# Linear attention into a SwiGLU block on one core: inputs as (head half, 64 chunks of 9 tokens)

## The chip, the cores and the metric

The kernel runs on one core of one Trainium2 chip. The metric is the device time of one execution in microseconds (us). TensorE (PE) has a 128x128 array with a weight load (PEld) ahead of each matmul; VectorE is DVE, ScalarE is ACT, GpSimd is POOL, and SyncE (SP) only issues DMAs here. Each engine takes its own instructions in program order, so an instruction that waits holds up all that stands behind it on its engine.

## What is computed

```python
q, k, v: (8, 8, 576, 64) float32          # batch, heads, tokens, head dim
def phi(x): return np.where(x > 0, x, np.exp(x) - 1.0) + 1.0      # elu(x) + 1
q_p, k_p = phi(q), phi(k)
kv  = np.einsum('bhsd,bhse->bhde', k_p, v)
z   = np.sum(k_p, axis=2)
num = np.einsum('bhsd,bhde->bhse', q_p, kv)
den = np.einsum('bhsd,bhd->bhs', q_p, z)[..., None] + 1e-06
x   = (num / den).transpose(0, 2, 1, 3).reshape(4608, 512)
g   = x @ w_gate                          # 512 x 1536
out = (g * sigmoid(g)) * (x @ w_val) @ w_out   # 1536 x 512, float32 out
```

## The kernel before

The 4608 tokens go through the block in nine groups of 512. Groups 0 to 7 are the first 512 tokens of each batch entry ("batch" below); group 8 holds the last 64 tokens of all eight (the tails).

**Layout.** A batch's k, q and v come as tiles of 128 partitions x 8 heads x (4 tokens x 64) float32: token `4p + j` on partition p, so each contiguous run is 1 KB. The tails come in pairs, 64 partitions each, in runs of 256 bytes. `load` (L96) issues all of it on SP: one DMA of 1 MB per tensor, and for every even batch two tail DMAs more. The output leaves on SP too. The weights come on POOL, cast to float16 on the way.

**Attention of a batch.** exp on ACT (L117), then `min(e,1) + max(x,0)` on DVE (L130, L133). `vcast` (ACT, L168) copies v to float16 with a column of ones beside each head, so that `mm1` (L186: 4 pieces of 128 tokens and a tail piece, for 4 head pairs: 20 matmuls of 129 columns) gives kv and z at once. `kv_copies` writes the kv blocks to `R` and the z columns to diagonal matrices, `zb` (L209) spreads z over the partitions by a matmul with ones. `s3_prod`, `s3_reduce`, `s3_recip`, `s3_scale` (DVE) give the denominators and scale q; `tr` transposes q by head pairs on PE, DVE copies it to `qT`; `mm2` (L271) multiplies by `R` and gives `xT`, the block's input.

**The block of a group.** `l1(g, fb)` for 12 slices of 128 hidden channels: 4 matmuls into `pG`, 4 into `pV` (512 columns each), Silu on ACT (L290), product on DVE (L291) into `hT`. Then `l2(g, t)` for 4 token pieces: 12 matmuls each into `pO`, evacuated, stored. `pG`, `pV`, `pO` and `pA` have two banks each.

**Order.** `manual_schedule`: the order on each engine is that of the code. Group g's l1 slices carry, by the table `chain`, the attention of batch g+1, and its l2 pieces, by `prep_a`, the exp and phi of batch g+2. The cast of v of batch g+2 stands at slices 4 to 7. Group 0 is different: the whole of batch 1 (`ch[8]` to `ch[11]`, then `pa`) and the phi of batch 2 go through in it. The loads of batch g+2 are issued at slice 0 of group g, behind the stores of group g-1 on SP.

```python
            if 4 <= fb < 8 and b2 < B:
                vcast(b2, [fb - 4])
```

Of the kernel before, what the change touches and what calls it, by code (L numbers as in the profile page):

```python
# [17 lines left out]
def kernel(  # L18
# [42 lines left out]
    kp = two([P, J, H * D], FP16, "kp")
    qp = two([P, J, H * D], FP16, "qp")
    ktp = two([P, H * D], FP16, "ktp")
    qtp = two([P, H * D], FP16, "qtp")
    vm = two([P, J, H, D + 1], FP16, "vm")
    vt = [two([P, H, D + 1], FP16, f"vt{i}") for i in range(2)]
    prod = sb.tile([P, 2, H * D], FP16, name="prod")
    prodt = sb.tile([P, H * D], FP16, name="prodt")
    den = sb.tile([P, J * H], FP32, name="den")
    rden = sb.tile([P, J * H], FP32, name="rden")  # L70
    dent = sb.tile([P, H], FP32, name="dent")
    rdent = sb.tile([P, H], FP32, name="rdent")
    zd = sb.tile([P, NH2, P], FP16, name="zd")
    zbc = sb.tile([P, H * D], FP16, name="zbc")
    R = [sb.tile([P, NH2, P], FP16, name=f"R_{b}") for b in range(B)]
    qT = two([P, NH2, NM], FP16, "qT")
    qTt = sb.tile([P, NH2, NM], FP16, name="qTt")
    xT = [two([P, NM], FP16, f"xT{c}") for c in range(NH2)]
    hT = two([P, FB, NM], FP16, "hT")
    sil = two([P, NM], FP16, "sil", 2)  # L80
    osb = two([P, 2, DM], FP32, "osb")
    wg = sb.tile([P, NH2, DF], FP16, name="wg")
# [22 lines left out]
    def load_k(b):
        load(b, k, k32, kt32)

    def load_q(b):
        load(b, q, q32, qt32)

    def load_v(b):
        load(b, v, v32, vt32)


    def exps(src, srct, e, et, b):
        for i in range(2):
            nc.scalar.activation(out=e[:, 4 * i:4 * i + 4, :], in_=src[b % 2][:, 4 * i:4 * i + 4, :],  # L117
                                 func=AF.Exp, bias=0.0, scale=1.0)
# [353 lines left out]
```

## Time and profile before

| | us |
|---|---|
| three timed runs | 430.30, 430.93, 432.88 (median 430.93) |
| the profiled execution | 431.02 |
| span of its trace | 429.30 |
| PE busy | 332.6 (77%) |
| DVE busy | 240.4 (56%) |
| ACT busy | 168.9 (39%) |
| DMA packets | 45,494, of which 13,728 under 512 bytes and 29,184 more under 2 KB |
| granted TensorE clock, mean | 0.936 |

Matmuls overlap in the array, so a row's duration is its latency, and the price of a matmul in a stream is the distance from start to start. An engine's busy share is a mean over stages with different limits; the stages are read apart below.

### The profile page before, as it was taken

What the parts mean: (1) busy time and instruction counts of PE and PEld (TensorE: products, weight loads), DVE (VectorE), ACT (ScalarE), POOL (GpSimd) and SP (SyncE); (2) the same over time, 40 slices, a digit from 0 to 9 for tenths busy, and PEclk for the clock granted to TensorE, in tenths of its full rate; (3) what the DMA queues carried; (4) which work ended last, traced back from release to release, by engine and by line L of the source; (5) the groups of instructions that cost most, each with busy time, mean ns of one, the idle gap of its engine ahead of it and who ended that gap; (6) DMA issues with size and microseconds to landing.
All of it is one profiled execution on the core that took longest, in us unless ns stands there. A gap on an engine that the chain in (4) does not pass through costs nothing.

```text
span 429.3 us, 4508 instructions
## 1 busy us (share of the span) xinstructions
PE 332.6 (77%) x1672; PEld 154.6 (36%) x1672; DVE 240.4 (56%) x430; ACT 168.9 (39%) x271; POOL 10.5 (2%) x26
## 2 busy tenths in 40 slices
PE   0329506386788995699879948998799999999995
PEld 0113202142334452245334523453345444444442
DVE  3583102467978663678576626786666772342431
ACT  3604006752344741564346513744365221321320
POOL 3420000000000000000000000000000000000000
PEclk9999856888899999799999996999899999999999
DMA  8899992001630069004701780046002002002004
GB/s 234 184 247 247 240 273 43 1 0 50 214 128 2 1 211 253 2 0 148 246 2 43 205 219 0 0 158 234 0 20 82 2 0 99 0 2 98 0 2 98
DMA packets 45494, 42.76 MB, mean 100 GB/s; under 512 B 13728, under 2 KB 42912, under 8 KB 45472
## 3 DMA queue, kind: packets, MB, share of 16 engines
q1 hardware_dynamic: 40720, 37.75, 30.4%
q0 software_dynamic: 4752, 4.72, 6.5%
q8 instruction: 13, 0.21, 0.2%
q14 instruction: 9, 0.07, 0.1%
HBM read 37.75 MB, written 9.44 MB: 110 GB/s over the span
## 4 chain that ended last, share of the span: by engine, by line
PE 52%; DMA 16%; SPq 15%; DVE 9%; ACT 4%; issue 3%; DVEq 0%; POOL 0%; ACTq 0%; POOLq 0%
PE pO_137 L297 11%; PE pO_138 L297 10%; SPq L102 10%; DMA v_0_67<-in_v_dram 7%; PE pG_133 L287 7%; PE pG_134 L287 7%; PE pV_135 L287 7%; PE pV_136 L287 6%; DMA v_1_68<-in_v_dram 5%; SPq L97 5%; DMA q_0_65<-in_q_dram 2%; DVE qp_81 L231 2%; DVE qp_82 L231 2%; DMA k_1_64<-in_k_dram 1%; DVE hT_121 L291 1%
## 5 line engine op out<-in xcount | busy, mean ns | idle before, releaser
L287 PEld LDWEIGHTS <-wg 128*128 128x128 f16 x432 | 42.5, 101 | 86.1 <-issue 43.9
L287 PEld LDWEIGHTS <-wv 128*128 128x128 f16 x432 | 43.5, 101 | 55.1 <-issue 7.3
L291 DVE SCALAR_TENSOR_TENSOR hT_120<-pV_136,sil_123 128x512 f16<-128x512 f32 x30 | 20.7, 689 | 61.3 <-ACT sil_123 L290 48.1
L290 ACT ACTIVATE sil_122<-pG_133 128x512 f16<-128x512 f32 x54 | 32.2, 597 | 53.2 <-PE pG_133 L287 53.1
L290 ACT ACTIVATE sil_123<-pG_134 128x512 f16<-128x512 f32 x54 | 32.1, 595 | 41.2 <-PE pG_134 L287 38.8
L287 PE MATMUL pG_134<-xT_0_112,wg 128*128 128x512 f16 x30 | 12.2, 408 | 32.9 <-ACT sil_123 L290 32.9
L291 DVE SCALAR_TENSOR_TENSOR hT_120<-pV_135,sil_122 128x512 f16<-128x512 f32 x30 | 20.7, 689 | 24.7 <-PE pV_135 L287 20.5
L297 PEld LDWEIGHTS <-hT_120 128*128 128x128 f16 x240 | 23.7, 100 | 28.4 <-issue 2.3
L303 ACT ACTIVATE osb_125<-pO_138 128x512 f32<-128x512 f32 x9 | 5.4, 597 | 65.9 <-PE pO_138 L297 65.9
L297 PE MATMUL pO_137<-wo,hT_120 128*128 128x512 f16 x120 | 29.2, 396 | 0.0
L291 DVE SCALAR_TENSOR_TENSOR hT_121<-pV_136,sil_123 128x512 f16<-128x512 f32 x24 | 16.5, 689 | 22.1 <-ACT sil_123 L290 11.6
L297 PE MATMUL pO_138<-wo,hT_120 128*128 128x512 f16 x120 | 27.5, 379 | 0.0
L297 PEld LDWEIGHTS <-hT_121 128*128 128x128 f16 x192 | 18.8, 98 | 22.6
L168 ACT ACTIVATE vm_87<-v_0_67 128x512 f16<-128x512 f32 x16 | 9.7, 625 | 42.5 <-DMA v_0_67<-in_v_dram 42.5
L291 DVE SCALAR_TENSOR_TENSOR hT_121<-pV_135,sil_122 128x512 f16<-128x512 f32 x24 | 16.5, 689 | 17.2 <-PE pV_135 L287 15.2
L297 PE MATMUL pO_137<-wo,hT_121 128*128 128x512 f16 x96 | 22.0, 379 | 0.0
L297 PE MATMUL pO_138<-wo,hT_121 128*128 128x512 f16 x96 | 22.0, 379 | 0.0
L221 DVE TENSOR_REDUCE den<-prod 128x16 f32<-128x1024 f16 x16 | 19.4, 1211 | 0.1
L301 DVE TENSOR_SCALAR osb_124<-pO_137 128x512 f32<-128x512 f32 x9 | 6.2, 691 | 17.9 <-PE pO_137 L297 17.9
L186 PE MATMUL pA_139<-vm_87,kp_79 128*128 128x129 f16 x32 | 4.6, 251 | 14.4 <-DVE kp_79 L133 13.7
L168 ACT ACTIVATE vm_88<-v_1_68 128x512 f16<-128x512 f32 x16 | 9.7, 625 | 8.5 <-DMA v_1_68<-in_v_dram 8.5
L252 PE MATMUL pA_139<-id_130,qp_81 128*128 128x128 f16 x32 | 3.8, 254 | 11.4 <-DVE qp_81 L231 11.3
(207 smaller groups left out, 663.2 us busy)
## 6 DMA issues: line engine op xcount, KB each, us to landing
k_0_63<-in_k_dram SPq DMA_DIRECT2D x4, 1024.0 KB, 6.8
v_0_67<-in_v_dram SPq DMA_DIRECT2D x4, 1024.0 KB, 9.6
q_0_65<-in_q_dram SPq DMA_DIRECT2D x4, 1024.0 KB, 9.9
k_1_64<-in_k_dram SPq DMA_DIRECT2D x4, 1024.0 KB, 7.2
q_1_66<-in_q_dram SPq DMA_DIRECT2D x4, 1024.0 KB, 9.6
v_1_68<-in_v_dram SPq DMA_DIRECT2D x4, 1024.0 KB, 11.4
out_dram<-osb_124 SPq DMA_DIRECT2D x8, 512.0 KB, 2.7
out_dram<-osb_125 SPq DMA_DIRECT2D x8, 512.0 KB, 3.3
```

The lines of the kernel that those rows point to most:

```text
L97: nc.sync.dma_start(out=main[b % 2][:, :, :], in_=src[b][:, 0:NM, :].rearrange("h (p j) d -> p h (j d)", j=J))
L102: nc.sync.dma_start(out=tail[(b // 2) % 2][TL * e:TL * e + TL, :, :], in_=src[b + e][:, NM:S, :].rearrange("h p d -> p h d"))
L168: nc.scalar.activation(out=vm[b % 2][:, j, :, 0:D], in_=v32[b % 2][:, :, D * j:D * j + D], func=AF.Copy, bias=0.0, scale=1.0)
L186: nc.tensor.matmul(out=o, lhsT=kp[b % 2][:, j, P * hp:P * hp + P], rhs=vm[b % 2][:, j, :, :].rearrange("p h c -> p (h c)")[:, 130 * hp:130 ...
L221: nc.vector.tensor_reduce(out=den[:, cs], in_=prod[:, :, :].rearrange("p j (h d) -> p (j h) d", h=H), axis=AX.X, op=ALU.add)
L231: nc.vector.tensor_tensor(out=qv, in0=qv, in1=rden[:, H * j:H * j + H].unsqueeze(2).to_broadcast([P, H, D]), op=ALU.mult)
L287: nc.tensor.matmul(out=ps[:, :], lhsT=w[:, cc, P * fb:P * fb + P], rhs=xT[cc][g % 2][:, :], start=(cc == 0), stop=(cc == NH2 - 1))
L290: nc.scalar.activation(out=s[:, :], in_=pG[i][:, :], func=AF.Silu, bias=0.0, scale=1.0)
L291: nc.vector.scalar_tensor_tensor(out=hT[g % 2][:, fb, :], in0=pV[i][:, :], scalar=SC, in1=s[:, :], op0=ALU.mult, op1=ALU.mult)
L297: nc.tensor.matmul(out=ps[:, :], lhsT=hT[g % 2][:, fb, P * t:P * t + P], rhs=wo[:, fb, :], start=(fb == 0), stop=(fb == FB - 1))
L301: nc.vector.tensor_scalar(out=o[:, t % 2, :], in0=ps[:, :], scalar1=1.0 / SC, scalar2=None, op0=ALU.mult)
L303: nc.scalar.activation(out=o[:, t % 2, :], in_=ps[:, :], func=AF.Copy, bias=0.0, scale=1.0 / SC)
```

## The change

**Layout.** A batch's tile is now 128 partitions = 2 head halves x 64 chunks; on a partition lie 4 heads x 9 tokens x 64. The contiguous run is 9 x 64 x 4 = 2304 bytes, 64 x 9 = 576 leaves no rest, and all tail tiles and their work are gone. Every tensor comes in four DMAs of 295 KB: two head pairs x two halves, the half of partitions 0 to 63 on SP, that of 64 to 127 on POOL.

**Groups.** 72 units (batch, token of the chunk) of 64 tokens in nine groups of 8 units. Group g holds the last g units of batch g-1 and the first 8-g of batch g; group 8 is the rest of batch 7.

**kv.** The contraction runs over 64 partitions: per head pair, 9 tokens x 2 halves = 18 matmuls of 129 columns on 64 rows of the array each, halves in turn, each half into its own bank: 36 a batch for 20. For batches 0 to 2, z comes by 18 matmuls of 256 columns from kp directly (`z_direct`), so that the denominators don't wait for v; later batches keep the diagonal way (2 matmuls of 256).

**Order.** Three tables: `early` for batches 1 and 2 (in groups 0 and 1), `late` for batch 3, `steady` for 4 to 7. One batch per group throughout. Casts of v of batch g+2 stand at slices 8 and 9 from group 1 on; the loads of batch g+2 are written at slice 4. mm2 stands after or between the l2 pieces (before: slices 10 and 11).

**Silu.** In slices 0 to 3 of groups 0 and 1 the gate is 0.5·g·(1 + tanh(g/2)): Tanh on ACT and one more DVE instruction.

**Banks.** `pV` has three, the attention shares three (`pX`, in turn), l2 uses banks of pV and pG. The copy of the transposed q is on ACT. Stores are of 64 rows of 2 KB.

```diff
-        nc.sync.dma_start(
-            out=main[b % 2][:, :, :],
-            in_=src[b][:, 0:NM, :].rearrange("h (p j) d -> p h (j d)", j=J))
...
+        v4 = src[b].rearrange("(a l) (c j) d -> a c l (j d)", a=2, j=J)
+        for hh, eng in ((0, nc.sync), (1, nc.gpsimd)):
+            eng.dma_start(out=dst[b % 2][C * hh:C * hh + C, 2 * lp:2 * lp + 2, :],
+                          in_=v4[hh][:, 2 * lp:2 * lp + 2, :])
...
+        for j in range(J):
+            for hh in range(2):
+                rows = slice(C * hh, C * hh + C)
                 nc.tensor.matmul(
+                    out=kvb[b][hh][:, 256 * lp:256 * lp + W], lhsT=kp[b % 2][rows, j, P * lp:P * lp + P],
+                    rhs=vm[b % 2][rows, j, :, :].rearrange("p l c -> p (l c)")[:, 130 * lp:130 * lp + W],
+                    start=(j == 0), stop=(j == J - 1))
...
+    def z_direct(b):
+        zps[b] = (bank(), bank())
+        for j in range(J):
+            for hh in range(2):
+                rows = slice(C * hh, C * hh + C)
+                nc.tensor.matmul(out=zps[b][hh][rows, 0:HL * D], lhsT=ones[rows, 0:C], rhs=kp[b % 2][rows, j, :],
+                                 start=(j == 0), stop=(j == J - 1))
...
+        if tanh:
+            nc.scalar.activation(out=s[:, :], in_=pg[:, :], func=AF.Tanh, bias=0.0, scale=0.5)
+            nc.vector.scalar_tensor_tensor(out=s[:, :], in0=s[:, :], scalar=1.0, in1=pg[:, :],
+                                           op0=ALU.add, op1=ALU.mult)
...
+    def early(b):
...
+        sl[0] = [lambda: exp_k(b, 0)]
+        sl[1] = [lambda: exp_k(b, 1)]
+        sl[2] = [lambda: exp_q(b, 0)]
+        sl[3] = [lambda: exp_q(b, 1)]
+        sl[4] = [lambda: phi_k(b, 0)]
+        sl[6] = [lambda: phi_k(b, 1)]
+        sl[7] = [lambda: z_direct(b)]
+        sl[8] = [lambda: phi_q(b, 0)]
+        sl[10] = [lambda: phi_q(b, 1)]
+        sl[11] = s3a(b, 0)
...
+    def steady(b):
...
+        sl[0] = [lambda: phi_q(b, 0), lambda: mm1(b, 0)]
+        sl[1] = [lambda: phi_q(b, 1), lambda: mm1(b, 1)]
+        sl[2] = [lambda: zdiag(b, 0), lambda: zdiag(b, 1), lambda: r_copies(b)]
+        sl[3] = [lambda: zb(b), lambda: zb_copy(b), lambda: s3_prod(b, 0)]
...
+            sl[8] = sl[8] + [lambda: vcast(b2, 0)]
+            sl[9] = sl[9] + [lambda: vcast(b2, 1)]
...
+            if fb == 4 and b2 < B:
+                ld_k(b2)
+                ld_q(b2)
+                ld_v(b2)
```

What stands in a row on ACT in the first slices of group 0, before (sil is the Silu of a slice, vm_87 the cast of batch 2's v, v_0_67 its float32 tile):

```order
L290 ACTIVATE sil_122<-pG_133 128x512
L168 ACTIVATE vm_87<-v_0_67 128x8x64
L290 ACTIVATE sil_123<-pG_134 128x512
L168 ACTIVATE vm_87<-v_0_67 128x8x64
L290 ACTIVATE sil_122<-pG_133 128x512
```

and now (L277 is the Tanh; k_1_64 and q_1_66 are batch 1's tiles):

```order
L126 ACTIVATE ek<-k_1_64 128x1152
L277 ACTIVATE sil_97<-pG_109 128x512
L126 ACTIVATE ek<-k_1_64 128x1152
L277 ACTIVATE sil_96<-pG_108 128x512
L126 ACTIVATE eq<-q_1_66 128x1152
L277 ACTIVATE sil_97<-pG_109 128x512
L126 ACTIVATE eq<-q_1_66 128x1152
L281 ACT_TABLE_LOAD
```

Batch 2's cast is gone from group 0; batch 1's exps stand in its place.

On SP, the loads from batch 1's q to batch 2's v, before (kt, qt, vt are tails):

```order
L97 DMA q_1_66<-in_q_dram 128x8x256
L97 DMA v_1_68<-in_v_dram 128x8x256
L97 DMA k_0_63<-in_k_dram 128x8x256
L102 DMA kt_1_70<-in_k_dram 64x8x64 x2
L97 DMA q_0_65<-in_q_dram 128x8x256
L102 DMA qt_1_72<-in_q_dram 64x8x64 x2
L97 DMA v_0_67<-in_v_dram 128x8x256
```

and now (L112 is a DMA of one element that makes SP wait for what it reads; each load has a twin for the other half on POOL):

```order
L112 DMA gate<-v_0_67 1x1
L96 DMA k_1_64<-in_k_dram 64x2x576 x2
L96 DMA q_1_66<-in_q_dram 64x2x576 x2
L112 DMA gate<-wv 1x1
L96 DMA v_1_68<-in_v_dram 64x2x576 x2
L96 DMA k_0_63<-in_k_dram 64x2x576 x2
```

The tails are gone, and batch 1's v is behind the last piece of w_val.

On ACT before group 0, now (zbc is z on all partitions, from the banks that `z_direct` fills):

```order
L126 ACTIVATE ek<-k_0_63 128x1152 x2
L207 ACTIVATE zbc<-pX_114 64x256
L207 ACTIVATE zbc<-pX_115 64x256
L126 ACTIVATE eq<-q_0_65 128x1152 x2
L152 ACTIVATE vm_75<-v_0_67 128x2x9x64 x2
```

The exps of q stand behind two copies that wait for PE.

## Rows read from the trace of the kernel before

**Rows 1.** Windows: head, groups 0 to 8, tail. Columns: stretch, length, busy, PEclk, DMA share, GB/s.

```profile
0.00:34.89 34.89, 7.89 (x41) 4.04 (x42) 20.96 (x43) 11.48 (x19) 10.51 (x26) 1.00 0.97 224
34.89:111.54 76.65, 42.05 (x190) 18.79 (x189) 29.22 (x51) 29.89 (x45) 0.00 (x0) 0.80 0.51 115
111.54:153.28 41.74, 37.10 (x189) 17.56 (x187) 33.11 (x60) 18.99 (x30) 0.00 (x0) 0.96 0.29 93
153.28:198.79 45.51, 36.88 (x190) 17.04 (x189) 28.79 (x54) 20.41 (x33) 0.00 (x0) 0.92 0.42 110
198.79:237.94 39.15, 34.87 (x187) 16.51 (x186) 27.11 (x49) 19.37 (x31) 0.00 (x0) 1.00 0.33 108
237.94:284.05 46.11, 38.90 (x190) 17.83 (x189) 28.79 (x54) 20.41 (x33) 0.00 (x0) 0.89 0.40 109
284.05:324.43 40.38, 36.39 (x187) 17.08 (x186) 27.12 (x49) 19.37 (x31) 0.00 (x0) 0.96 0.32 104
324.43:361.15 36.72, 35.25 (x190) 16.73 (x189) 23.41 (x44) 11.70 (x21) 0.00 (x0) 1.00 0.07 29
361.15:393.17 32.02, 32.02 (x178) 15.04 (x177) 11.57 (x17) 8.96 (x15) 0.00 (x0) 1.00 0.09 34
393.17:424.24 31.07, 31.07 (x145) 13.97 (x143) 10.37 (x15) 7.76 (x13) 0.00 (x0) 1.00 0.14 38
424.24:429.30 5.06, 0.17 (x1) 0.00 (x0) 0.00 (x0) 0.60 (x1) 0.00 (x0) 1.00 0.36 80
```

**Rows 2.** Waits: who waited for whom; us in total, times, longest.

```profile
ACT vm_87 L168 <- DMA v_0_67<-in_v_dram: 42.5, 4, 22.7
PE pG_134 L287 <- ACT sil_123 L290: 36.4, 5, 20.1
```

**Rows 3.** Timeline of SP: start, time in the issue, line, what it fills.

```profile
32.26 12.37 SPq L102 DMA_DIRECT2D kt_1_70<-in_k_dram  x2
...
45.34 12.87 SPq L102 DMA_DIRECT2D qt_1_72<-in_q_dram  x2
58.26 0.84 SPq L97 DMA_DIRECT2D v_0_67<-in_v_dram  x1
```

**Rows 4.** Windows: a stretch in which DMAs of 1 KB runs move.

```profile
4.00:6.00 2.00, 0.00 (x0) 0.00 (x0) 0.00 (x0) 0.00 (x0) 0.36 (x2) 1.00 1.13 337
```

**Rows 5.** Groups of instructions: shapes, count, busy us, mean ns of one.

```profile
L133 DVE SCALAR_TENSOR_TENSOR kp_79<-k_0_63,ek 128x512 f16<-128x512 f32 x16 | 10.1, 686 | 0.1
L130 DVE TENSOR_SCALAR eq<-eq 128x2048 f16<-128x2048 f16 x8 | 5.5, 692 | 1.5 <-ACT eq L117 1.5
L117 ACT ACTIVATE ek<-k_0_63 128x1024 f16<-128x1024 f32 x8 | 8.0, 1048 | 5.0 <-DMA k_0_63<-in_k_dram 5.0
L216 DVE TENSOR_TENSOR prod<-qp_81,zbc 128x1024 f16<-128x1024 f16 x8 | 5.3, 662 | 0.0
L221 DVE TENSOR_REDUCE den<-prod 128x16 f32<-128x1024 f16 x16 | 19.4, 1211 | 0.1
L227 DVE RECIPROCAL rden<-den 128x16 f32<-128x16 f32 x16 | 4.0, 253 | 0.5
L231 DVE TENSOR_TENSOR qp_81<-qp_81,rden 128x512 f16<-128x512 f16 x16 | 10.4, 673 | 0.1
```

**Rows 6.** Timeline of PE: start, latency, line, tile, count; group 0's start, group 6's mm1.

```profile
34.89 0.63 PE L287 MATMUL pG_133<-xT_0_112,wg 128*128 128x512 f16 x1
...
37.02 0.51 PE L287 MATMUL pV_135<-xT_0_114,wv 128*128 128x512 f16 x1
...
326.15 0.39 PE L186 MATMUL pA_139<-vm_88,kp_80 128*128 128x129 f16 x4
...
327.29 0.38 PE L287 MATMUL pG_134<-xT_0_112,wg 128*128 128x512 f16 x1
```

**Rows 7.** Timeline: the last matmul of a slice and the product behind it.

```profile
342.95 0.38 PE L287 MATMUL pV_135<-xT_0_118,wv 128*128 128x512 f16 x1
...
343.44 0.69 DVE L291 SCALAR_TENSOR_TENSOR hT_120<-pV_135,sil_122 128x512 f16<-128x512 f32 x1 [1.10 <-PE pV_135 L287]
```

More of the change, by code (lines that the diff above doesn't have):

```diff
@@ L61 @@
[L61 to L82, printed above, removed]
@@ L105, in load_k @@
[L105 to L118, printed above, removed]
-        if b % 2 == 0:
-            nc.scalar.activation(out=et[:, :, :], in_=srct[(b // 2) % 2][:, :, :],
-                                 func=AF.Exp, bias=0.0, scale=1.0)
@@ new lines, in r_copies @@
+    def r_copies(b):
+        for hh in range(2):
+            kvv = kvb[b][hh][:, :].rearrange("p (i c) -> p i c", i=2)
+            for h2 in range(2):
+                rows, c = slice(D * h2, D * h2 + D), (D + 1) * h2
+                nc.scalar.activation(
+                    out=R[b % 2][rows, :, D * h2:D * h2 + D].rearrange("p (l a) c -> p a l c", a=2)[:, hh, :, :],
+                    in_=kvv[rows, :, c:c + D], func=AF.Copy, bias=0.0, scale=1.0)
+    zps = {}
+    def zb(b):
+        zps[b] = (bank(),) * 2
+        for hh in range(2):
+            nc.tensor.matmul(out=zps[b][hh][C * hh:C * hh + C, 0:HL * D], lhsT=ones[:, 0:C],
+                             rhs=zd[:, 2 * hh:2 * hh + 2, :].rearrange("p i c -> p (i c)"), start=True, stop=True)
@@ new lines, in units, with mm2 @@
+    def units(g):
+        return [(u // J, u % J) for u in range(U * g, U * g + U)]
+    def mm2(g, i, eng):
+        ps = bank()
+        us = units(g)
+        for b in sorted(set(u[0] for u in us)):
+            js = [j for (bb, j) in us if bb == b]
+            c0 = C * us.index((b, js[0]))
+            nc.tensor.matmul(out=ps[:, c0:c0 + C * len(js)], lhsT=R[b % 2][:, i, :],
+                             rhs=qT[b % 2][:, i, js[0]:js[-1] + 1, :].rearrange("p j c -> p (j c)"),
+                             start=True, stop=True)
+        dst = xT[i][g % 2][:, :]
+        if eng == "A":
@@ new lines @@
+    ld_k(0)
+    ld_q(0)
+    nc.gpsimd.iota(out=idx[:, :], pattern=[[-1, P]], base=0, channel_multiplier=1)
+    ld_v(0)
+    nc.gpsimd.memset(ones[:, :], 1.0)
+    ld_w1(0)
+    sp_after(v32[0][0:1, 3, 0:1].bitcast(FP16)[:, 0:1], 0)
+    ld_k(1)
+    ld_q(1)
+    ld_w1(1)
+    ld_w1(2)
+    for i in range(3):
+        ld_w2(i)
+    sp_after(wv[0:1, 0, DF - 512:DF - 511], 1)
+    ld_v(1)
+    nc.vector.tensor_scalar(out=id16[:, :], in0=idx[:, :], scalar1=0.0, scalar2=None, op0=ALU.is_equal)
+    for i in range(2):
+        nc.vector.memset(vm[i][:, :, :, D:D + 1], 1.0)
+        nc.vector.memset(R[i][:, :, :], 0.0)
@@ new lines, with s3a @@
+    A, V = "A", "V"
+    for lp in range(2):
+        exp_k(0, lp)
+        phi_k(0, lp)
+    z_direct(0)
+    for lp in range(2):
+        exp_q(0, lp)
+        phi_q(0, lp)
+    for lp in range(2):
+        vcast(0, lp)
+        mm1(0, lp)
+    r_copies(0)
+    for c in range(3):
+        s3_prod(0, c)
+        s3_reduce(0, c)
+        s3_recip(0, c)
+        s3_scale(0, c)
+        tr(0, c)
+        tr_copy(0, c, A)
+    for i in range(4):
+        mm2(0, i, A if i % 2 else V)
+    def s3a(b, c):
+        return [lambda: s3_prod(b, c), lambda: s3_reduce(b, c)]
```

495 lines of the change are left out of this document (217 added, 278 removed).

## Prediction

> **What bounds the kernel now.** I read the page, then the windows cut where each group's first l1 matmul starts, then the waits, then the timelines. PE is the engine with the most work, but the windows show that it bounds only the end: group 8 is 144 matmuls of 512 columns and nothing else and takes 31.07, so 0.2157 apiece; group 7 adds 0.9 of mm2 [rows 1]. Group 6, which carries one batch's attention and no casts of v, takes 36.72. All other groups are longer: group 0 takes 76.65 with PE busy 42.05, groups 2 and 4 take 45.5 and 46.1, and in just these the granted clock falls, to 0.80, 0.92 and 0.89 [rows 1]. The waits name the reason: ACT waits 42.5 in all, four times, 22.7 at worst, for v to land before its cast, and PE waits 36.4, five times, 20.1 at worst, for a Silu that stands behind that cast [rows 2]. On SP one sees why v is late in group 0: the tails of k and q hold the queue for 12.37 and 12.87, and v is issued only at 58.26 [rows 3]. So group 0 is bound by the transfers, groups 2 and 4 (the batches that bring tails) by the same wait on a smaller scale, the end by PE, and the head (34.89, DVE busy 20.96 [rows 1]) by a serial chain over DVE.
>
> **The head.** The input of batch 0 is 3 x 1.18 = 3.54 MB. Runs of 1 KB moved at 337 GB/s [rows 4], and 2304-byte runs should not be slower; the lowest rate of a long stretch is the head's 224, tails and all [rows 1]. Counted from time 0 at that mean, which has the start-up in it, k is in by 5.3, q by 10.5, v by 15.8; I take k's second pair at 5.8, as little moves at first, and its first pair at 4.1. Now the chain. An exp covers 1152 columns: 1.048 x 1152/1024 = 1.18. A phi of one pair is a min (0.692 x 1152/2048 = 0.39) and two sums (0.686 x 576/512 = 0.77), so 1.93 [rows 5]. phi of k: 5.3 to 9.2. z_direct: 18 matmuls of 256 columns; at group 0's start 512 columns went every (37.02 - 34.89)/5 = 0.426 [rows 6], so 0.213 each, 3.8 in all, to 13.2 with its latency; two small copies, 14.0. Only then ACT comes to q (the order rows in the section on the change): exps to 16.3, phi of q to 19.0. One s3 third is 0.662 + 1.211 at three quarters, 0.42 for the two short ones (0.253 is one of them), and 0.673 x 1.5 [rows 5]: 2.85, with gaps 2.95; three give 27.9. Six transposes 0.9, the copy 0.8, then four mm2 and a copy, 2.3: l1 starts at 31.9, 3.0 earlier. The kv part (v at 15.8 at the latest, cast behind the exps by 18.7, 36 matmuls, copies by 24) lies beside it. The bound below is z_direct with its two halves at once (1.9 less); above, a slower load costs nothing until q comes after 14, and at 224 GB/s it comes by 10.5.
>
> **The transfers in group 0.** All that is needed, in order, at the low rate of 224: batch 0 by 15.8, first weight pieces and batch 1's k, q (3.4 MB) by 31, second weights (1.05) 35.7, third 40.4, w_out (1.57) 47.4, v of batch 1 52.7, batch 2 68.5. Needed at about 32, 40, 47, 56, 62 and 75. So the 20.1 wait goes; what would be late next is the second weight piece, with some 4 us of room. Batch 2's cast is no longer in group 0.
>
> **A group's sum.** 31.07 is fixed. mm1 before: 20 matmuls between 326.15 and 327.29, 0.057 each [rows 6]. The trace has no matmul on 64 rows; bounds are 0.028 (two halves at once) and 0.10 (a weight load of 128 columns not hidden; half of 0.2157 for 128 columns twice). I take 0.057, since the columns are the same: 36 cost 2.05. 18 transposes of 128 columns at the same price 1.03, mm2 0.86, zb 0.22. Sum 35.2 (with z_direct at 0.108 x 18 = 1.94 instead of zb: 36.95).
>
> *Steady, groups 3 to 6.* A slice's product starts 0.27 after its last matmul's slot (342.95 + 0.216, 343.44 [rows 7]). Walking the tables with that and the prices above: DVE does phi of q (3.9) beside two slices, then the diagonals, and is level with PE at zb; PE waits 0.2 for the first scale, 0.25 for the second, 0.3 for the third xT at the border: 0.8. Group 6 of before, of like build, has 36.72 - (31.07 + 40 x 0.057 + 0.22 + 0.86) = 2.3 of waits. I take 1.3 between them: 36.5. DVE's 27 to 29 and ACT's 19 to 20 in such groups of before [rows 1] hardly change, so neither bounds. The loads: SP comes free of the last store two DVE copies (0.69 each, as in [rows 7]) after the group's start, at 1.4, the cast of v is reached after slice 8, at about 18.7; 1.77 MB in 17.3 us need 102 GB/s. POOL's half has a whole group more, since nothing stands before it on POOL but loads.
>
> *Early, groups 0 and 1.* 36.95, and: z_direct waits 1.1 for the second phi of k (DVE is busy with it 1.93 after a product), the first transposes 1.9 for s3's first third, which starts only after slice 11, the second 0.5, the border 0.8, as mm2 stands last with three banks: 41.3. Group 0 starts at the low clock: five matmuls at 0.426 for 0.2157, 1.2 more [rows 6]: 42.5. The tanh products add 4 x 0.69 to DVE beside slices that leave it 1 us each: nothing. Without that cover they cost 2.8.
>
> *Late, group 2.* 35.2, and mm1 waits 1.1 for phi of k, the first transposes 1.0, mm2 0.9 for the last qT copy, the border 0.8: 39.0.
>
> Groups 7 and 8 have nothing new: 32.0 and 31.1. The tail is kept at 5.1 (smaller last stores against one more in the queue).
>
> Sum: 31.9 + 42.5 + 41.3 + 39.0 + 4 x 36.5 + 32.0 + 31.1 + 5.1 = 368.9 of span. The profiled execution took 431.02 for a span of 429.3, 1.7 more, and stands within 0.1 of the median of the runs: 370.6, about 371. Against before, group 0 gives 34, the casts of v in groups 2 and 4 some 16, the head 3, the rest little; group 6 gives nothing.
>
> **Rivals.** *The two halves overlap in the array.* Then z_direct and mm1 cost half: 1.9 in the head, 2.0 in each of groups 0 and 1, 1.0 in each of five more: 10.9 less, 360. For it: halves alternate and have their own banks; against it: each still has its own weight load, and no row shows such a pair. The Trainium skill (TensorEngine Tiling (Array Packing), Key Properties) says that tiles run loads and matmuls in parallel, and that a change of tiling drains the engine; by the first half of the rule the time is this rival's, by the second a little above the forecast. No row here shows either.
>
> *Group 0 still waits.* If the weights share the engines badly with SP's and POOL's loads, one wait like the longest of before, 20.1 [rows 2], remains: 391. Against it: the 8 us of tails and the 3.8 MB of batch 2 ahead are gone.
>
> *v is late again.* SP's half fills only 64 partitions; below 102 GB/s the cast waits. At before's price (groups 2 and 4 against 3: 6.7 each [rows 1]) in groups 1 to 5: 404.
>
> *POOL starves, and it is slower.* Half of every batch now hangs on POOL's descriptors. Its weight DMAs in the head were issued with DVE at 20.96 of 34.89 busy [rows 1], and no later POOL work exists to read. To end above 431 each of groups 1 to 5 must lose 12 more, after a lead of a group: POOL would need over 48 us for 1.77 MB, 37 GB/s. The Trainium skill (SBUF — State Buffer, Who interferes with whom) has this mechanism: VectorE in a two-port mode locks GpSimd out and a DMA issued there lacks descriptors; by it the min of phi, 0.39 at a time, would hold POOL up, and the loads with it. No row shows a POOL DMA that was held so.
>
> **How the numbers follow.** Forecast 371 (own range 363 to 381): 0.58. Overlap, 360: 0.16. Group 0 waits, 391: 0.09. v late, 404: 0.12. POOL, above 426: 0.05. The range for 8 in 10 takes the first three: 357 to 392. About 1% is what a measurement of this kernel can tell from no change: faster 0.95, same 0.01, slower 0.04.
>
> **What would show it.** Right: no wait of PE on a Silu above 3; group 0 at 41 to 45; four groups near 36.5 at clock 1.00; l1 from about 32. Wrong: an ACT wait for v or for k in group 0 or at slices 8 and 9; mm1 pairs at under 0.06 for two (overlap) or at 0.2 (drain); transposes that wait above 2 for the scale; POOL's loads landing behind SP's.

## The result, and the profile after

The changed kernel takes 364.22 us in the median of 4 runs (363.87 to 367.16); the kernel before took 431.90 in 4 runs beside it. The ratio is 0.845 with a 95% interval of 0.839 to 0.851: between the medians 67.7 us, between 15 and 16% of the time, are gone. Forecast were 371 and, as the range, 357 to 392. The profiled execution took 364.31 for a span of 362.5. Its windows, cut where each group's first l1 matmul starts (columns as in [rows 1]):

```profile
0.00:31.87 31.87, 8.56 (x77) 6.04 (x78) 17.98 (x34) 12.83 (x17) 14.01 (x26) 1.00 1.02 237
31.87:73.53 41.66, 37.74 (x225) 17.74 (x224) 28.83 (x48) 20.64 (x31) 7.79 (x13) 1.00 1.07 250
73.53:114.59 41.06, 36.43 (x225) 17.38 (x224) 29.17 (x49) 29.31 (x39) 3.59 (x6) 1.00 0.46 113
114.59:151.61 37.02, 35.15 (x211) 16.61 (x208) 29.56 (x55) 20.75 (x31) 5.18 (x8) 1.00 0.59 136
151.61:187.21 35.60, 35.39 (x210) 16.61 (x208) 27.00 (x49) 21.54 (x31) 3.57 (x6) 1.00 0.56 132
...
294.05:326.35 32.30, 32.10 (x150) 14.49 (x149) 10.97 (x16) 10.75 (x18) 0.00 (x0) 1.00 0.14 33
...
```

The rows left out are groups 4 to 6 (35.62, 35.61 and 35.61), group 8 (31.08) and the tail (5.07). Beside the forecast, in us:

| | before | after | forecast | after less forecast |
|---|---|---|---|---|
| head | 34.89 | 31.87 | 31.9 | 0.0 |
| group 0 | 76.65 | 41.66 | 42.5 | -0.8 |
| group 1 | 41.74 | 41.06 | 41.3 | -0.2 |
| group 2 | 45.51 | 37.02 | 39.0 | -2.0 |
| groups 3 to 6 | 39.15, 46.11, 40.38, 36.72 | 35.6 each | 36.5 each | -3.6 |
| groups 7, 8, tail | 68.15 | 68.45 | 68.2 | +0.3 |

So group 0 gave 35.0, groups 2 and 4 gave 8.5 and 10.5, groups 3 and 5 gave 3.6 and 4.8, the head 3.0, groups 1 and 6 some 1 each. A steady group now keeps PE busy for 35.39 of 35.60 at a granted clock of 1.00; in groups 0, 2 and 4 of before the clock stood at 0.80, 0.92 and 0.89, in groups 1 and 5 at 0.96 [rows 1].

The waits of PE in the changed kernel (who waits for whom; total, times, longest):

```profile
PE pX_114 L203 <- DVE kp_71 L132: 11.5, 1, 11.5
PE pX_113 L166 <- ACT vm_75 L152: 4.1, 1, 4.1
PE pX_114 L238 <- DVE qp_73 L227: 4.0, 2, 2.1
```

The 36.4 of PE behind a Silu, 20.1 at worst [rows 2], are gone without a successor; the two longest waits lie in the head, and after it no wait of PE is longer than 2.0. Batch 2's v is now issued and cast so (timelines of SP and of ACT: start, time, line, tile):

```profile
45.09 1.28 SPq L96 DMA_DIRECT2D v_0_67<-in_v_dram  x2
```

```profile
106.04 2.23 ACT L152 ACTIVATE vm_75<-v_0_67 128x1152 f16<-128x1152 f32 x2
```

In [rows 3] it was issued at 58.26, with ACT already waiting for it; now there are 61 us between the issue on SP and the cast, in the second l2 piece of group 1.

### The profile page after: what moved, and what is told of

It is laid out like the page before. It is cut to its first block, busy times and chain, and to the rows that moved or that the text cites. A ratio compares the mean times of both kernels' runs of the same rounds, so it can differ in the third digit from the quotient of the medians.

```text
span 362.5 us, 5036 instructions
## 1 busy us (share of the span) xinstructions
PE 322.8 (89%) x1856; PEld 152.2 (42%) x1856; DVE 230.6 (64%) x401; ACT 180.5 (50%) x265; POOL 36.5 (10%) x63
## 4 chain that ended last, share of the span: by engine, by line
PE 72%; DVE 15%; issue 5%; ACT 4%; DMA 2%; POOL 0%; DVEq 0%; ACTq 0%; POOLq 0%
PE pG_108 L273 11%; PE pG_109 L273 10%; PE pV_110 L273 7%; PE pV_111 L273 7%; PE pV_112 L273 7%; PE pG_109 L292 6%; PE pV_111 L292 6%; PE pG_108 L292 5%; PE pV_110 L292 5%; DVE den L216 2%; DMA k_0_63<-in_k_dram 2%; DVE hT_94 L282 1%; DVE qp_73 L227 1%; DVE prod L212 1%; DVE qp_73 L132 1%
## 5 line engine op out<-in xcount | busy, mean ns | idle before, releaser
L273 PEld LDWEIGHTS <-wg 128*128 128x128 f16 x432 | 40.6, 98 | 49.4 <-issue 5.9
L281 ACT ACTIVATE sil_96<-pG_108 128x512 f16<-128x512 f32 x50 | 29.9, 597 | 37.7 <-PE pG_108 L273 35.4
L281 ACT ACTIVATE sil_97<-pG_109 128x512 f16<-128x512 f32 x50 | 29.9, 597 | 35.8 <-PE pG_109 L273 32.5
L292 PEld LDWEIGHTS <-hT_95 128*128 128x128 f16 x192 | 18.6, 98 | 21.1
L216 DVE TENSOR_REDUCE den<-prod 128x12 f32<-128x768 f16 x24 | 22.7, 947 | 0.3
L292 PE MATMUL pG_109<-wo,hT_94 128*128 128x512 f16 x60 | 13.8, 379 | 0.0
L292 PE MATMUL pV_110<-wo,hT_94 128*128 128x512 f16 x60 | 13.8, 379 | 0.0
L292 PE MATMUL pG_108<-wo,hT_94 128*128 128x512 f16 x60 | 13.8, 379 | 0.0
L292 PE MATMUL pV_111<-wo,hT_94 128*128 128x512 f16 x60 | 13.8, 379 | 0.0
L203 PE MATMUL pX_114<-kp_71,ones 64*64 64x256 f16 x9 | 2.1, 413 | 11.5 <-DVE kp_71 L132 11.5
L273 PE MATMUL pG_108<-xT_0_90,wg 128*128 128x512 f16 x30 | 11.6, 387 | 0.4 <-DVE xT_0_90 L266 0.4
L273 PE MATMUL pG_108<-xT_0_86,wg 128*128 128x512 f16 x30 | 11.7, 390 | 0.0
L273 PE MATMUL pG_108<-xT_0_92,wg 128*128 128x512 f16 x30 | 11.6, 387 | 0.0
L273 PE MATMUL pG_108<-xT_0_88,wg 128*128 128x512 f16 x30 | 11.6, 387 | 0.0
L132 DVE SCALAR_TENSOR_TENSOR qp_73<-q_0_65,eq 128x576 f16<-128x576 f32 x16 | 11.4, 755 | 0.3
L227 DVE TENSOR_TENSOR qp_73<-qp_73,rden 128x768 f16<-128x768 f16 x12 | 11.4, 954 | 0.2
L132 DVE SCALAR_TENSOR_TENSOR kp_71<-k_0_63,ek 128x576 f16<-128x576 f32 x16 | 11.4, 755 | 0.3
L132 DVE SCALAR_TENSOR_TENSOR kp_72<-k_1_64,ek 128x576 f16<-128x576 f32 x16 | 11.4, 755 | 0.3
L132 DVE SCALAR_TENSOR_TENSOR qp_74<-q_1_66,eq 128x576 f16<-128x576 f32 x16 | 11.4, 755 | 0.3
L282 DVE SCALAR_TENSOR_TENSOR hT_94<-pV_110,sil_96 128x512 f16<-128x512 f32 x10 | 6.9, 690 | 7.3 <-ACT sil_96 L281 4.6
```

The lines of the kernel that those rows point to most:

```text
L132: nc.vector.scalar_tensor_tensor(out=dst[b % 2][:, :, D * l:D * l + D], in0=src[b % 2][:, l, :].rearrange("p (j d) -> p j d", d=D), scalar ...
L203: nc.tensor.matmul(out=zps[b][hh][rows, 0:HL * D], lhsT=ones[rows, 0:C], rhs=kp[b % 2][rows, j, :], start=(j == 0), stop=(j == J - 1))
L216: nc.vector.tensor_reduce(out=den[:, 12 * c:12 * c + 12], in_=prod[:, :, :].rearrange("p j (l d) -> p (j l) d", d=D), axis=AX.X, op=ALU.add)
L227: nc.vector.tensor_tensor(out=qv, in0=qv, in1=rden[:, 12 * c:12 * c + 12].unsqueeze(2).to_broadcast([P, 12, D]), op=ALU.mult)
L273: nc.tensor.matmul(out=ps[:, :], lhsT=w[:, chan(i), P * fb:P * fb + P], rhs=xT[i][g % 2][:, :], start=(i == 0), stop=(i == 3))
L281: nc.scalar.activation(out=s[:, :], in_=pg[:, :], func=AF.Silu, bias=0.0, scale=1.0)
```

## The experiments

### Where group 0's 35 us came from: the place of the cast

**e5_before_cast_last** moves one thing in the kernel before.

```diff
-            if 4 <= fb < 8 and b2 < B:
+            if 4 <= fb < 8 and 1 <= g and b2 < B:
                 vcast(b2, [fb - 4])
 ...
         if g == 0:
             run(pa2[0][2:])
             for x in pa2[1:]:
                 run(x)
+            vcast(2, [0, 1, 2, 3])
+            vcast_tail(2)
```

> The kernel before, with the cast of batch 2's v moved from slices 4 to 7 of group 0 to the end of group 0; tails and queue as they were. Theory (what cost group 0 its 35 us is only the place of this cast, ahead of Silus on ACT): no wait of PE on a Silu above 3 is left in group 0, group 0 shortens from 76.65 by the 20.1 of that wait, groups 2 and 4 keep theirs; about 411. Rival (the transfers bound group 0, by whatever wait): v of batch 1 or the k of batch 2 is waited for instead, and the time stays above 425.

Measured: 411.11, against 432.43 for the kernel before beside it (ratio 0.951, 0.946 to 0.956). Windows, groups 0 and 1:

```profile
34.24:89.95 55.71, 41.53 (x191) 18.96 (x190) 29.24 (x51) 27.69 (x41) 0.00 (x0) 0.85 0.70 158
89.95:131.69 41.74, 37.05 (x189) 17.55 (x187) 33.11 (x60) 21.32 (x35) 0.00 (x0) 0.96 0.28 93
```

Group 0 falls by 20.9 to 55.71, group 1 stays at 41.74 and groups 2 to 8 at their lengths to within 0.4. No byte and no matmul was saved; only five casts stand later in ACT's order. The theory holds, and nothing took the wait's place: the longest waits of PE left in group 0 are 4.7 for phi of k and 3.9 for the scale, and before had them too.

**e7_cast_in_group0** is the counterpart in the changed kernel.

```diff
+        if g == 0:
+            sl[4] = sl[4] + [lambda: vcast(2, 0)]
+            sl[5] = sl[5] + [lambda: vcast(2, 1)]
...
```

(The hunk left out takes the two casts of batch 2 out of group 1's l2 blocks.)

> The changed kernel with one thing undone: batch 2's v is cast in slices 4 and 5 of group 0 again, instead of in the four l2 blocks of group 1. Theory (the place of the cast counts by itself, whatever the layout): SP issues batch 2's v at 45 to 46 and POOL at 52, it lands at 57 to 62, ACT waits from 43 until then, PE waits 13 to 17 for a Silu; 378 to 382. Rival (without tails v comes in time): group 0 stays at 42 to 45, 364 to 367.

Measured: 386.33 (ratio 0.892, 0.887 to 0.898), 22 more than the changed kernel; above both ranges, and on the theory's side. Waits (total, times, longest):

```profile
PE pG L273 <- ACT sil L281: 18.5, 1, 18.5
ACT vm L152 <- DMA v<-in_v_dram: 19.2, 1, 19.2
```

Without tails, on two queues and in the new layout, v of batch 2 lands at 63.15 and ACT waits 19.2 for it: nearly the wait of before. I had put the landing at 57 to 62. Group 0 takes 62.03, 20.4 more. So the new layout does not bring v in time; the new order no longer needs it in time.

**e6_before_no_tail_loads** keeps the order of before and takes the tails' DMAs out.

```diff
-        if b % 2 == 0:
+        if False:
             for e in range(2):
                 nc.sync.dma_start(out=tail[(b // 2) % 2][TL * e:TL * e + TL, :, :],
...
+    for t in kt32 + qt32 + vt32:
+        nc.gpsimd.memset(t[:, :, :], 0.0)
```

> The kernel before without the DMAs of the tails (the tail tiles are set to zero once, so the tail rows of the output are not computed from the inputs); the order is kept. Theory (the tails held the SP queue): v of batch 2 is issued by about 37 instead of 58 and lands before slice 4 needs it, so group 0 loses 20, groups 2 and 4 lose 6.7 each: about 398. Rival (the sheer bytes in the first 70 us make v late; the tails are small): group 0 loses at most the 8 us that the tails' own bytes took, and groups 2 and 4 at most 2 each: about 420.

Measured: 415.73 (ratio 0.963, 0.958 to 0.967). Neither number came; 415.73 is nearer to the rival's 420. The timeline of SP, and of ACT where batch 2's v is cast (in brackets, idle time and what ended it):

```profile
14.87 8.18 SPq L97 DMA_DIRECT2D v<-in_v_dram  x1
...
35.62 14.04 SPq L97 DMA_DIRECT2D v<-in_v_dram  x1
```

```profile
59.84 0.63 ACT L168 ACTIVATE vm<-v 128x512 f16<-128x512 f32 x1 [18.64 <-DMA v<-in_v_dram]
```

SP comes to batch 2's v at 35.62, as the theory said, but then that one DMA holds it for 14.04, and v lands 24 us after SP came to it. ACT still waits 18.64. Group 0 gains 4.3 (76.65 to 72.33), the head 3.0, groups 2 and 4 gain 3.4 and 5.6, groups 3 and 5 lose 1.1 and 0.8. The tails cost what they cost in groups 2 and 4 and in the head, but the long wait of group 0 was not theirs.

**e10_before_no_tails** puts e5 and e6 together and takes away the attention work on the tails too (their exps, phi, casts, small matmuls, normalisation and transposes).

> The kernel before with batch 2's cast at the end of group 0 and without the attention work on the tails and its loads (the ninth group still runs, on zeros, so the tail rows are left out). Theory (tails cost more than their loads: exps, phi, products, casts and the two small matmul sets lie on the path of every group): group 0 at 50 to 53, groups 1 to 5 at 38 to 39.5 each, 380 to 386. Rival (only the tails' loads cost anything): the sum of the two single edits, 411 less 17, 394 to 398.

Measured: 391.35 (ratio 0.907, 0.901 to 0.912), nearer to the rival's 394 to 398 than to 380 to 386. Group 0 takes 57.28, so the tails have no share in what is left of it; groups 1 to 5 take 40.07, 38.98, 40.37, 38.58 and 41.15. From e5 the tails are worth 16.0 between the two profiled spans, and 19 by the ratios of the runs (0.951 and 0.907), since e10's profiled execution was the longest of its four and e5's the shortest. What holds groups 3 and 5 at 40 to 41 without any tail is shown by ACT and PE at slice 4 of group 5 (timelines) and PEclk behind it (windows; PEclk is the third figure from the end):

```profile
260.56 0.63 ACT L168 ACTIVATE vm<-v 128x512 f16<-128x512 f32 x1 [4.79 <-DMA v<-in_v_dram]
```

```profile
261.73 1.02 PE L290 MATMUL pG<-xT,wg 128*128 128x512 f16 x4 [2.27 <-ACT sil L293]
...
266.68 1.91 PE L290 MATMUL pG<-xT,wg 128*128 128x512 f16 x4
268.39 1.77 PE L290 MATMUL pV<-xT,wv 128*128 128x512 f16 x4
270.00 1.03 PE L290 MATMUL pG<-xT,wg 128*128 128x512 f16 x4
```

```profile
261.00:264.00 3.00, 2.27 (x8) 0.69 (x7) 2.29 (x3) 3.00 (x7) 0.00 (x0) 0.84 0.00 0
264.00:266.00 2.00, 0.64 (x5) 0.35 (x4) 1.96 (x6) 0.20 (x1) 0.00 (x0) 0.50 0.00 0
268.00:270.00 2.00, 2.00 (x7) 0.72 (x6) 0.00 (x0) 0.60 (x1) 0.00 (x0) 0.53 0.00 0
```

v is asked for at slice 4 and lands 4.79 later; PE waits 2.27, and then its clock is at half until about 270. The four wg matmuls at 266.68 take until 268.39, 1.71 where 0.86 is usual, the next four 1.61. The wait of 2.27 thus costs 1.6 more in slow matmuls, and beside it PE waits 1.06 and 0.58 for DVE's scale: together the 5.5 by which this group is longer than its counterpart in the changed kernel. The lower clock does not follow each such wait. In group 2 PE waits 1.9 for a Silu behind v and 2.3 for the scale, in group 3 it waits 1.8 and 2.3; the clock falls in group 3 alone, and that group is 1.4 longer (windows):

```profile
128.05:167.03 38.98, 34.74 (x183) 16.29 (x182) 25.75 (x46) 18.74 (x30) 0.00 (x0) 1.00 0.34 108
167.03:207.40 40.37, 36.25 (x182) 16.69 (x181) 25.83 (x46) 18.74 (x30) 0.00 (x0) 0.96 0.32 105
```

### What the early start of batch 1 brings, and what tanh is for

**e8_batch1_late** keeps all of the changed kernel but the place of batch 1's preparation; with the exps gone from its first slices, group 0 runs on Silu alone.

```diff
             sl, w = early(b1)
+            if g == 0:
+                old = sl
+                sl = [[] for _ in range(FB)]
+                sl[8] = sum(old[0:4], []) + old[4]
+                sl[9] = old[6] + old[8]
+                sl[10] = old[7] + old[10]
+                sl[11] = old[11]
 ...
-            l1(g, fb, tanh=(g < 2 and fb < NT))
+            l1(g, fb, tanh=(g == 1 and fb < NT))
```

> The changed kernel with batch 1's preparation back where the kernel before had it: its exps and phi in slices 8 to 11 of group 0, group 0 with Silu alone; everything else, batch 2's cast too, as in the changed kernel. Theory (the rest of group 0's gain, what is left once batch 2's cast has moved, is the early start of batch 1): group 0 takes 53 to 57 instead of 41.7, the other groups do not change; 375 to 380. Rival (the rest of the gain is the layout): group 0 stays within 3 of 41.7; 364 to 367.

Measured: 371.63 (ratio 0.857, 0.852 to 0.862), below the theory's range and above the rival's. Windows, group 0:

```profile
32.01:79.53 47.52, 39.42 (x226) 18.72 (x224) 26.41 (x44) 23.32 (x33) 7.82 (x13) 0.93 0.97 221
```

Group 0 takes 47.52, 5.9 more; its longest wait of PE is 6.5 for phi of k before z_direct. That is half of what I expected: the order of the last four slices explains 5.9 of the 15.6 between e10's group 0 and the changed kernel's, and the other 9.7 are open.

**e3_silu_only** sets `NT = 0`, so that Silu stands beside the exps.

> The changed kernel with Silu in place of tanh and product in the first four slices of groups 0 and 1, so that ACT changes its table between Silu and Exp in each of them. Theory (tanh gate is needed, since the exps lie in these slices): two table loads of 1.28 beside 0.60 and 1.16 make 4.3 of ACT in each of four slices that last 1.73 on PE, so each of the two groups takes 8 to 10 more; 380 to 384. Rival (ACT catches up before anything waits for it): 364 to 367.

Measured: 384.63 (ratio 0.886, 0.881 to 0.891), 0.6 above the theory's range. Windows of groups 0 and 1, and a piece of ACT's timeline:

```profile
31.84:83.86 52.02, 41.78 (x225) 18.75 (x224) 25.96 (x44) 31.34 (x39) 7.93 (x13) 0.90 0.86 199
83.86:135.09 51.23, 40.65 (x225) 18.43 (x224) 26.42 (x45) 37.68 (x45) 3.61 (x6) 0.90 0.37 90
```

```profile
34.61 1.28 ACT L126 ACT_TABLE_LOAD   x1
35.91 1.16 ACT L126 ACTIVATE ek<-k 128x1152 f16<-128x1152 f32 x1
37.09 1.28 ACT L281 ACT_TABLE_LOAD   x1
38.38 0.60 ACT L281 ACTIVATE sil<-pG 128x512 f16<-128x512 f32 x1
```

Each of the two groups grows by 10.2 to 10.4. A pair of table changes, with its exp and its Silu, takes 4.39 from one pair to the next (34.61 to 39.00), where a slice of PE lasts 1.73. The tanh gate is worth 20 us. That this is so only because the exps were moved into these slices is argued: in e8 group 0 has Silu alone and its exps in one slice, and grows by 5.9 with their later start included.

### Whether the halves overlap, and what it is worth

**e1_halves_apart** swaps two loops in mm1 and, in the same way, in z_direct, so that nine matmuls on one half are followed by nine on the other.

```diff
-        for j in range(J):
-            for hh in range(2):
+        for hh in range(2):
+            for j in range(J):
...
```

> The changed kernel with the matmuls of the two 64-row halves one half after the other (nine, then nine) in kv and in z_direct, instead of alternating. Theory (alternating halves run at once in the array): 18 kv matmuls cost 1.0 again instead of 0.5, so 1.0 more in each of seven groups, 1.0 more for z_direct in groups 0 and 1, 1.9 more in the head at the low clock: 10.8 more, about 375. Rival (a matmul on 64 rows is cheap by itself, no overlap needed): no change, 364.

Measured: 370.00 (ratio 0.856, 0.852 to 0.860), 5.8 above the changed kernel's median; the profiled span is 367.5, 5.0 above the changed kernel's. That is half of the theory's 10.8, and well above the rival's 364. Timelines of PE, the changed kernel in group 3, then e1 in group 3, then the kernel before in group 6:

```profile
153.65 0.38 PE L273 MATMUL pV_110<-xT_1_93,wv 128*128 128x512 f16 x1
153.96 0.23 PE L166 MATMUL pX_115<-vm_75,kp_71 64*128 64x129 f16 x1
153.96 0.23 PE L166 MATMUL pX_113<-vm_75,kp_71 64*128 64x129 f16 x1
154.03 0.22 PE L166 MATMUL pX_115<-vm_75,kp_71 64*128 64x129 f16 x1
154.03 0.22 PE L166 MATMUL pX_113<-vm_75,kp_71 64*128 64x129 f16 x1
...
154.43 0.22 PE L166 MATMUL pX_113<-vm_75,kp_71 64*128 64x129 f16 x1
154.57 0.39 PE L273 MATMUL pG_109<-xT_1_87,wg 128*128 128x512 f16 x1
```

```profile
156.54 0.59 PE L273 MATMUL pV<-xT,wv 128*128 128x512 f16 x2
157.07 0.98 PE L166 MATMUL pX<-vm,kp 64*128 64x129 f16 x18
157.99 0.61 PE L273 MATMUL pG<-xT,wg 128*128 128x512 f16 x2
```

```profile
325.94 0.38 PE L287 MATMUL pV_135<-xT_0_118,wv 128*128 128x512 f16 x1
326.15 0.39 PE L186 MATMUL pA_139<-vm_88,kp_80 128*128 128x129 f16 x4
```

Alternating, the halves start in pairs at the same time, a pair every 0.058 (the last of the nine starts at 154.43), and 18 of them put 0.70 between the l1 matmuls around them (153.65 + 0.22 to 154.57). One half by itself goes no faster: its matmuls too start every 0.058, where a matmul on 128 rows costs 0.057 [rows 6]. So a matmul on half the rows is not cheaper by itself; two that alternate cost as one. The Trainium skill (TensorE: Matmul & The Clock Gate, Why this matters for your kernels) says this of matmuls on 32 rows: one alone takes the time of a full one, and the gain is in running tiles at once. This trace agrees, on 64 rows.

Apart, the 18 put 1.02 there (156.54 + 2 x 0.216 to 157.99). That this is just 18 x 0.057 is chance, for two things in it cancel. First, apart the halves still overlap in part: the 18 start within 0.77 (0.98 less the 0.22 that the last one lasts), and 17 steps of 0.058 would be 0.99. Second, the change from 128 rows to 64 and back has a price. To the nanosecond, the first pair starts 0.312 after the start of the l1 matmul ahead of it (153.65 to 153.96) and the next l1 matmul 0.148 after the last pair; in the kernel before, with 128 rows throughout, the same two distances are 0.216 (325.94 to 326.15) and 0.057. So each row of 64-row matmuls costs 0.19 beside its nine steps of 0.058. Against e1 the overlap is worth 0.4 to 0.6 in a group's mm1, 0.5 in z_direct of groups 0 and 1, and 0.7 in the head; against halves with no overlap at all, which no run has, it would be more.

### Whether the second queue matters

**e2_one_queue_later** issues POOL's half on SP from batch 2 on.

```diff
-        for hh, eng in ((0, nc.sync), (1, nc.gpsimd)):
+        for hh, eng in ((0, nc.sync), (1, nc.gpsimd if b < 2 else nc.sync)):
```

> The changed kernel with both halves of every load from batch 2 on issued on SP; the first two batches as before it. Theory (from group 0 on the second queue is worth nothing): SP issues 12 DMAs of 0.63 each per group, some 4 more than now, and the last lands well before slice 8 of the group; 364. Rival (POOL's lead of a group is what hides the loads): ACT waits for v at slice 8 of groups 2 to 5, some 2 to 6 in each; 372 to 388.

Measured: 362.94 (ratio 0.837, 0.831 to 0.842), not above the changed kernel. Group 3 takes 35.61 as in the changed kernel, and ACT's waits for v come to 1.1 in all. Its profiled execution, at 365.48 the longest of its five, shows the clock once more: group 1 has the wait of 2.0 for phi of k that the changed kernel has too, but here the clock is at 0.74 from 88 to 92 and 0.83 from 92 to 96, and the group takes 42.69 for 41.06. The theory holds from batch 2 on: the loads have a group's time and one queue does. By the Trainium skill (DMA: Bandwidth & Descriptors, Issuing engines are not separate DMA queues) a second issuing engine saves only the time of issuing; the run agrees. For the head and batch 1, where POOL also carries the weights, the queues were not tried apart.

### Two versions that are shorter still

**e4_q_first** moves z_direct's two copies of batch 0 behind the exps of q on ACT.

```diff
...
     z_direct(0)
     for lp in range(2):
         exp_q(0, lp)
         phi_q(0, lp)
+    z_copy(0)
...
```

> The changed kernel with one thing moved: in the head, batch 0's exps of q stand ahead of z_direct's two copies on ACT instead of behind them. Theory (DVE's four idle us before phi of q come from that order): the exps of q run at 10.5 to 13.5 as the pairs land, phi of q ends at 15.6 instead of 19.5, group 0's first l1 matmul starts at about 28.0 instead of 31.9, and the groups keep their lengths; 360.3. Rival (k's and q's landing or the weights bind the head next): the start moves by less than 1.5, or group 0 grows by what the head loses; 363 to 365.

Measured: 361.54 (ratio 0.834, 0.829 to 0.840). Timelines of ACT in the head, the changed kernel, then e4:

```profile
13.57 0.38 ACT L207 ACTIVATE zbc<-pX_114 64x256 f16<-64x256 f32 x1 [4.12 <-PE pX_115 L203]
...
14.37 2.22 ACT L126 ACTIVATE eq<-q_0_65 128x1152 f16<-128x1152 f32 x2
```

```profile
10.98 1.16 ACT L126 ACTIVATE eq<-q 128x1152 f16<-128x1152 f32 x1 [1.22 <-DMA q<-in_q_dram]
13.69 1.16 ACT L126 ACTIVATE eq<-q 128x1152 f16<-128x1152 f32 x1 [1.55 <-DMA q<-in_q_dram]
14.76 0.76 ACT L209 ACTIVATE zbc<-pX 64x256 f16<-64x256 f32 x2
```

The 4.12 of ACT waiting for PE with q behind it are gone, but the second pair of q lands only at 13.69, where 12.3 was assumed. l1 starts at 29.29 instead of 31.87: 2.6 of the 3.9 expected, since the landing of q binds next.

**after_again** and **e4_again** set the two side by side.

> The changed kernel again, unaltered, as the measure for the two versions that run beside it: 363.9 to 367.2, as in its own runs.

> The version with batch 0's exps of q ahead of z_direct's copies, beside the changed kernel itself. Theory (the head is really shorter): 2.5 to 4 below the changed kernel of the same round of runs. Rival (the first comparison was a difference between runs): within 1 of it.

Measured: 364.58 (ratio 0.844, 0.840 to 0.848) and 361.34 (0.839, 0.835 to 0.843). The difference of the medians is 3.2, within the expected 2.5 to 4; the two intervals still touch, but the head is 2.5 to 2.6 shorter in both pairs of traces.

**e9_group1_late** also brings the steady order one group forward.

```diff
-        if g < 2:
+        if g < 1:
             sl, w = early(b1)
-        elif g == 2:
+        elif g == 1:
             sl, w = late(b1)
 ...
+        if g == 0:
+            pre[0] = [lambda: exp_k(2, 0), lambda: exp_k(2, 1), lambda: exp_q(2, 0), lambda: exp_q(2, 1)]
...
```

(In `early`, the casts of batch 1's v go to slices 9 and 10 and those of batch 2's take their place in the second l2 block; tanh stays in group 0; batch 3's phi of k moves into group 1's l2 blocks.)

> The version with q first, and one group earlier in the steady order: batch 2's exps and cast of v stand in group 0's l2 blocks (batch 1's cast in its slices 9 and 10), group 1 takes the order of group 2, group 2 the steady one, and tanh stays in group 0 alone. Theory (the order of work sets each group's length, and ACT has the room in group 0's l2 blocks): group 1 falls from 41.1 to 37.0, group 2 from 37.0 to 35.6, group 0 grows by at most 0.5; 5 below the version with q first, 355 to 357. Rival (batch 2's v or k is not there by 57 to 63): ACT waits in group 0's l2 blocks, group 0 grows by 4 or more, 359 to 362.

Measured: 360.05 (ratio 0.834, 0.830 to 0.838), the lowest median of all and clear of the changed kernel beside it. From e4_again (361.34, ratio 0.835 to 0.843) it is not clear, and its profiled span is the longer of the two (359.2 against 358.8). Windows of groups 0 to 2, and ACT:

```profile
29.30:75.59 46.29, 40.09 (x225) 18.65 (x224) 28.69 (x48) 28.35 (x38) 7.86 (x13) 0.93 1.06 239
75.59:112.71 37.12, 35.14 (x209) 16.48 (x208) 29.52 (x55) 20.73 (x31) 4.98 (x8) 1.00 0.60 134
112.71:148.32 35.61, 35.40 (x211) 16.53 (x209) 26.99 (x49) 21.54 (x31) 3.58 (x6) 1.00 0.56 131
```

```profile
53.96 1.18 ACT L152 ACTIVATE vm<-v 128x1152 f16<-128x1152 f32 x1 [3.07 <-DMA v<-in_v_dram]
...
67.52 1.18 ACT L152 ACTIVATE vm<-v 128x1152 f16<-128x1152 f32 x1 [2.10 <-DMA v<-in_v_dram]
```

Groups 1 and 2 give 3.9 and 1.4, as the theory had it, and the rival came true as well. ACT waits for v in group 0: 3.07 for batch 1's at slice 9, which lands at 53.96, and 2.10 for batch 2's in the l2 blocks. Group 0 grows by 5.5 (46.29 against e4's 40.80 in the same set) at a clock of 0.93. Of 5 expected, 1.3 is left between the medians and nothing between the spans. It is the mistake of the kernel before on a smaller scale. The half of batch 1's v that comes late is POOL's, which is issued there behind the weights. Issues in the changed kernel (KB each, us from issue to landing; the first at 27.35, the others at 40.91 and 41.58):

```profile
v_1_68<-in_v_dram POOLq DMA_DIRECT2D x1, 288.0 KB, 26.0
v_1_68<-in_v_dram SPq DMA_DIRECT2D x2, 288.0 KB, 6.9
```

POOL's first piece lands at 53.4, SP's two at 47 to 49. The changed kernel casts batch 1's v only in its l2 blocks, so there nothing waits for it.

## Why the prediction was right, and where it was not

**The total.** 364.2 lies in the range and in the forecast's own range of 363 to 381; the span came out 6.4 below the sum (362.5 against 368.9). It lies nearer to the overlap rival's 360 than to the forecast's 371. Every period stands within 2.0 of its term, and the signs of being right came out: no wait on a Silu, group 0 between 41 and 45, four equal groups at clock 1.00, l1 from 31.9. Two signs of being wrong came too: pairs of mm1 at 0.058, which is the overlap, and a load of POOL's that landed behind SP's, batch 1's v, which cost nothing here.

**Group 0: right number, wrong reason in one step.** The step "the tails of k and q hold the queue" named them as what made v late. e6 takes them away and v is still 18.6 late; e7 has none and v is 19.2 late. The "8 us of tails" of the rival stand in no row; without the tails' loads group 0 is 4.3 shorter. The cause is the place of the cast: the loads of batches 0 and 1 and the weights are issued ahead of batch 2's v, which in three kernels landed between 59.8 and 67.3 whatever the layout, while ACT stood ready for the cast at 41 to 45. The sentence that carried the number was the last of that part, "Batch 2's cast is no longer in group 0"; e5 shows it alone to be worth 20.9. That all needed loads come in time in their new order held: no group waits for v or k.

**Groups 2 and 4: the same confusion, smaller.** The forecast gave the casts of v there some 16. Measured over the whole change are 19.0 (8.5 and 10.5); e6 gives 9.0 of it to the tails' loads. For the rest, e10 shows the same wait for v at slice 4 without tails, 4.0 to 4.8 of ACT in each of groups 2 to 5, and its price has two parts: the wait of PE itself, and at times the half clock behind it. The forecast's 16 was a difference of lengths of groups and had both in it. But the clock does not fall in groups 0, 2 and 4 alone, as the prediction read [rows 1]: groups 1 and 5 stand there at 0.96. That the changed kernel asks for v at slice 8, after a load issued at the group's start, is the difference that stands in the code; slice 8 without the new layout was not tried.

**The steady groups: two terms too large, two too small.** 36.5 were forecast, 35.6 came. mm1 was put at 2.05, and the overlap rival's mechanism is real, so it costs 1.4 (twice 0.70). Waits were put at 1.3 from before's group 6; the trace leaves 0.2 to 0.4, so half of that group's 2.3 was no fair guide to this build. Against it, 18 transposes cost 1.35 for 1.03 and zb 0.33 to 0.50 for 0.22 (their share of the time between the large matmuls around them in groups 3 to 6). The sum, -0.65 - 0.95 + 0.3 + 0.3, is about the -0.9 measured.

**The overlap rival.** It had 0.16 and 10.9 us. The mechanism came true, the price in part: e1 measures 5.0 to 5.8. The sum had taken one row's 0.057 for each of 36 matmuls. Nine pairs cost half of that, 0.52, but the change from 128 rows to 64 and back adds 0.19, which the 360 left out, and so 0.70 stands where it had 0.51. So both things that the prediction weighed there came: halves at once, and a price at the change of tiling.

**The head: two errors that cancel.** k's second pair was put at 5.8 and came at 8.29, and phi of k ended 2.2 later than forecast (11.4 for 9.2); z_direct, put at 3.8, took 2.1 in overlapping pairs. s3 started at 19.5 for 19.0, a third of s3 took 2.93 for 2.95, and l1 started on the tenth, by luck. The mean rate of 224 GB/s was near right for the head as a whole (237) and wrong for its first tensor: up to 8.29 the mean from time 0 is 183, since nothing moves in the first 2 us, and 0.34 of the 1.52 MB moved by then are not k.

**The early groups and the late one.** Group 1 is right to 0.2 (in groups 0 and 1 PE waits 2.1 and 2.2 for the scale and 1.5 and 2.0 for phi of k, where 2.4 and 1.1 were walked). Group 2 was put at 39.0 with 3.8 of waits; the trace shows 2.2.

**The other rivals.** Group 0 has no successor to its wait, v is late nowhere, and POOL starves nobody: it waits for buffers (21.4 at worst) and for its own earlier transfers (5.7), and after the head no engine that computes waits for a load. e2 shows that from batch 2 on POOL's queue is not needed at all, so that the risk given to it, and the benefit of the two queues, were both empty there. No run here shows a load of POOL's that an instruction of DVE held up.

**What stays open.** Of the 66.8 us of span, e5 places 20.9 (the cast), e10 less e5 16.0 (the tails; 19 by the ratios), e8 5.9 (batch 1's early start). The remaining 24 (some 21 by the ratios) lie almost all between e10 and the changed kernel: 9.7 in group 0 and 15.2 in groups 2 to 5 of the profiled executions. The mechanism in groups 2 to 5 is shown (v at slice 4, the scale, then in groups 3 and 5 the clock). In group 0 only the waits are: those of PE are 13.1 in e10 (4.1 for phi of k, 3.7 for the scale and 2.2 for batch 1's cast at the longest) at a clock of 0.82, 8.1 in e8 at 0.93, and 3.9 in the changed kernel at 1.00. Which part of the new layout or order shortens each of them was not tried.
